# Query and key matmuls in pairs of 256 columns for an even count of instructions, and one remainder visit in the second product

## The chip, the cores and the metric

The kernel runs on one core of one Trainium2 chip. The metric is the device time of one execution in microseconds (us), the median of several runs. A profile is one execution recorded by the hardware profiler; its span is a little shorter than the device time of the same execution.

The engines are named as in the profile: PE is TensorE's matmuls, PEld its weight loads, DVE is VectorE, ACT is ScalarE, POOL is GpSimd, SP is the engine that issues most DMAs. Every matmul here is two TensorE instructions, a weight load and the matmul itself.

## The reference

One transformer layer over x of 2048 rows and 640 columns. First comes an attention that passes a memory from segment to segment, then a feed-forward part; both take a layer norm of their input and add their result to it.

```python
mem = mem0                                    # 8 rows
for s in range(64):                           # segments of 32 rows, one after the other
    h = concatenate([mem, xs[s]])             # 40 rows of 640, xs from layernorm(x)
    q, k, v = h @ Wq, h @ Wk, h @ Wv          # 32 heads of 128
    scores = q @ k.T * 128 ** -0.5            # 40 x 40 a head
    p = softmax(where(mask, scores, -1e9))    # memory rows see all, the others are causal
    o = (p @ v) @ Wo                          # 40 rows of 640
    mem = o[:8]                               # goes into the next segment
    outs.append(o[8:])
h = x + concatenate(outs)
h2 = h + (relu(layernorm(h) @ w1 + b1) ** 2 @ w2 + b2)     # 640 -> 1728 -> 640
```

All arrays are bf16; products accumulate in 32 bits.

## The kernel before

The weights of the attention stay in on-chip memory (`wq`, `wk`, `wv`, `wo`). The order of all instructions is written out by hand: the Python code issues them in the order in which each engine runs them.

**A segment** is one call of `step(b, sp)`. Its 32 "main" rows are the 8 memory rows and 24 of the segment's own rows; the other 8 rows, the "tail", of four segments are projected together ahead of time. The projections go through `proj`: 128 x 32 weights (the transposed rows `hT`) against 512 columns of `wq`, `wk` or `wv`. For each of the five chunks `c` of the 640 inputs, four matmuls `k` = 0 to 3 write the output partitions 32k to 32k + 31 of one PSUM tile, so four of them use the four column groups of the array. A call for one half (`n`) of the heads is 20 matmuls. The order of a segment on TensorE is:

- `project`: queries of half 0, keys of half 0, queries of half 1 (tile `px`), keys of half 1;
- `scores(0)` (L505), the first two chunks of the values of half 0, `token_scores(0)` (L601), the rest of those values, `scores(1)`, `token_scores(1)` and the values of half 1 (tile `px`);
- some work from the list `fill`, `values(0)` (L551, L556: 20 matmuls of 32 or 128 columns), fill, four of the sixteen rounds of the output product (`wo_rounds`, L270, tile `pw`), `values(1)`, the other twelve rounds;
- while ACT and DVE bring the new memory from `pw` into `hT` (`wo_out`, L285 to L287, and `mem_to_hT`, L387): the rest of the fill, and `token_values` of the segment before (L426, L431: 40 matmuls of 32 columns).

`scores(0)` waits for the keys and queries; the first query matmul of the next segment waits for `hT`. `fill` holds the tail projections and the output product of finished tails; `portion` deals them out to the segments, so a segment has between 723 and 771 TensorE instructions, counted from one `scores(0)` to the next.

**The start** (`start`) projects the first tails and the first segment while the weights are still being loaded; `stream` does the queries and then the keys, chunk by chunk.

**The feed-forward part** goes in four passes of 512 rows. The first product (L1008; L1012 for its last, smaller block) makes 1728 = 13 x 128 + 64 hidden columns. The second product (L1060) has four quarters `q` in each pass: row blocks `pr` and `pr + 2`, and half `hf` of the output columns; each quarter is 2 x 13 matmuls of 320 columns. The last 64 hidden columns are the remainder, `rest` (L1037): the row blocks lie in two halves of 64 partitions, so two of its matmuls use two row halves of the array. It is run at the end of quarters 0 and 2, for that quarter and the next. Its tiles come from the pool `yps`; `mm` (three PSUM tiles) serves the first product, and `chn` (one) is free in this part. `y_out` adds the residual on DVE and issues the store.

Of the kernel before, what the change touches and what calls it, by code (L numbers as in the profile page):

```python
# [11 lines left out]
F32 = mybir.dt.float32  # L12
# [4 lines left out]
def kernel(  # L17
# [16 lines left out]
    nc = tc.nc  # L34
    _, S, D = A_x.shape
    _, H, E = A_Wq.shape
    M = A_mem0.shape[1]
    SEG = 32
    G = 4
# [68 lines left out]
    def head(p):  # L108

        n, g, j = p // 16, p // 4 % 4, p % 4  # L110
        return g * HG + j * 2 + n
# [85 lines left out]
    def ln_transpose(b):  # L197
# [23 lines left out]
            nc.scalar.copy(out=rows_in(b).rearrange("p c (s t) -> p c s t", s=4)[:, :, :, 0:HD], in_=ptv[:, :, :, 0:HD])  # L221
        return out

    def proj(w, by, lhs, n, ps, c0, c1):

        if by == "columns":
            wr = w[:].rearrange("p (c g j n k e) -> p c n k g j e", c=DC, g=G, n=2, j=4, k=4)
        elif by == "half":
            wr = w[:].rearrange("p (c k j n e) -> p c n k j e", c=DC, k=G, n=2, j=4)
        else:  # L230
            wr = w[:].rearrange("p (c n g k f) -> p c n k g f", c=DC, n=2, g=2, k=4)
        for c in range(c0, c1):
            for k in range(4):
                nc.tensor.matmul(ps[32 * k:32 * k + 32, :], lhsT=lhs(c), rhs=wr[:, c, n, k], start=(c == 0), stop=(c == DC - 1))  # L234

    def mmtile():
        return mm.tile([128, 512], F32, tag="mm", name="ps")
# [10 lines left out]
    def rowtile():  # L248
        return s2.tile([128, 512], BF16, tag="row", name="row", bufs=4)
# [12 lines left out]
    def wo_rounds(lhs, pw, hs):  # L262

        for h in hs:
            for kh in range(2):
                for ch in range(2):
                    j = kh * 2 + ch
                    p = h // 8 * 16 + kh * 8 + h % 8
                    c0 = 32 * (1 - kh)
                    nc.tensor.matmul(pw[32 * j:32 * j + 32, c0:c0 + DH], lhsT=lhs(p), rhs=wov2[:, head(p), ch],  # L270
                                     start=(h == 0), stop=(h == 15))

    def wo_out(pw, then=None, between=None):
# [145 lines left out]
    def token_values(s, v, vt4, po):  # L419

        sp = s % 4
        pTk, pTx = back.pop()
        for i in range(HG):
            for g in range(G):
                r = slice(32 * g, 32 * g + 32)
                nc.tensor.matmul(po[0][g][:, i * 32:(i + 1) * 32], lhsT=v[r, i * E:(i + 1) * E], rhs=pTk[r, i, :],  # L426
                                 start=(i == 0), stop=False, skip_group_check=True)
        for u in range(2):
            for g in range(G):
                r = slice(32 * g, 32 * g + 32)  # L430
                nc.tensor.matmul(po[0][g][:, u * 128:(u + 1) * 128].rearrange("p (j q) -> p j q", q=32)[:, :, 0:TL],  # L431
                                 lhsT=vt4[r, sp, u, :], rhs=pTx[r, u], start=False, stop=True, skip_group_check=True)

    def token_out(s, po):
# [27 lines left out]
    def step(b, sp, v=None):  # L462
# [11 lines left out]
        def project(which, w, dst, n, between=None):  # L474
            if ready:
                if between:
                    between()
                return
            if which + str(n) == "q1":
                ps = potile(1)  # L480
            elif which + str(n) == "k0" and not last:
                ps = chn.tile([128, 512], F32, tag="ch", name="pk0")[:]
            else:
                ps = mmtile()
            proj(w, "columns", lhs, n, ps, 0, DC)
            row = rowtile()
            if not between:
                evac_row(which, row[:], ps[:])
                flip(row[:], dst, n)
                return  # L490
            for u in range(2):
                nc.scalar.copy(out=row[:, u * 256:(u + 1) * 256], in_=ps[:, u * 256:(u + 1) * 256])  # L492
            between()
            for u in range(2):
                nc.vector.transpose(out=dst[:, n * 16 + u * 8:n * 16 + u * 8 + 8, 0:32],
                                    in_=row[:, u * 256:(u + 1) * 256].rearrange("p (h e) -> p h e", e=32))
# [3 lines left out]
        def scores(n):  # L500
            sm = chn.tile([128, 512], F32, tag="ch", name="sm")
            for j in range(4):
                for g in range(G):
                    p = n * 16 + g * 4 + j
                    nc.tensor.matmul(sm[32 * g:32 * g + 32, 0:NK], lhsT=qz[:, p, :], rhs=kT[:, p, :],  # L505
                                     start=(j == 0), stop=(j == 3), skip_group_check=True)
            sms[n] = sm

# [37 lines left out]
        def values(n, pB, po):  # L546
            cols = po[:, 0, 0:128]
            for j in range(4):
                i = n * 4 + j
                for k in range(4):  # L550
                    nc.tensor.matmul(cols[32 * k:32 * k + 32].rearrange("p (g i m) -> p i g m", g=G, i=4)[:, j],  # L551
                                     lhsT=v[:, i * E + 32 * k:i * E + 32 * k + 32],
                                     rhs=pB[:, :, SEG + j * M:SEG + (j + 1) * M],
                                     start=(j == 0), stop=False, skip_group_check=True)
            for k in range(4):
                nc.tensor.matmul(cols[32 * k:32 * k + 32].rearrange("p (g a) -> p g a", g=G), lhsT=vt4[:, sp, n, 32 * k:32 * k + 32], rhs=pB[:, :, 0:SEG],  # L556
                                 start=False, stop=True, skip_group_check=True)

        def values_out(n, po):
            evac(False, oT[:, n * 16:(n + 1) * 16, SEG:NK], po[:, 0, 0:128].rearrange("p (a m) -> p a m", m=M))  # L560

        project("q", wq, qT, 0)
        if not last and not ready:
            spread(0)
# [32 lines left out]
        def token_scores(n):  # L597
            skv = view()
            for j in range(4):
                for g in range(G):  # L600
                    nc.tensor.matmul(skv[32 * g:32 * g + 32, n * 4 + j, :], lhsT=qT[:, n * 16 + g * 4 + j, :],  # L601
                                     rhs=kT[:, n * 16 + g * 4 + j, :], start=True, stop=True,
                                     skip_group_check=True)

# [208 lines left out]
    def start():  # L813
# [23 lines left out]
        def stream(which, w, dst, turn=None):  # L837
            pas = [pop.tile([128, 2, 512], F32, tag="po%d" % h, name="pa%d" % h) for h in range(2)]
            for c in range(DC):
                for n in range(2):  # L840
                    proj(w, "columns", main, n, pas[0][:, n, :], c, c + 1)
                for n in range(2):
                    proj(w, "columns", lambda c: tail_rows(0, c), n, pas[1][:, n, :], c, c + 1)
                if c == 2 and turn:
                    turn()
                if c < DC - 1:
                    run(units, 7 + c % 2)
            run_late(0, 100)
            for n in range(2):
                row = rowtile()[:]  # L850
                evac_row(which, row, pas[0][:, n, :])
                tail_out(0, which, n, pas[1][:, n, :])
                flip(row, dst, n)
                run_late(0, 100)
                if which == "k":
                    tails_in(0, 0, n)

        stream("q", wq, qT, lambda: ln_transpose(("t", 2))())
        for n in range(2):
            spread(n)  # L860
        tails_v_in(0, nc.gpsimd, 0, 1)
# [133 lines left out]
    for t in range(S // NT):  # L995
# [32 lines left out]
            popx.close()  # L1028
            yps = ctx.enter_context(tc.tile_pool(name="yps", bufs=2, space=bass.MemoryType.PSUM))

        def ytiles():
            return [yps.tile([128, 512], F32, tag="y%d" % hh, name="y%d" % hh) for hh in range(2)]

        def rest(y, pr, cs, first):
            for hh in range(2):
# [14 lines left out]
        for q in range(NK4):  # L1050
            pr, hf = q // 2, q % 2
            cs = slice(hf * DH, (hf + 1) * DH)
            y = y1 if hf else ytiles()
            if more:
                for k in ((0, 1), (2,), (3,), ())[q]:
                    prep_turn(t + 1, k, prep_norm(t + 1, k, hts[k], *mvs[k]))
            for hh in range(2):
                k = pr + 2 * hh
                for fc in range(FFULL):
                    nc.tensor.matmul(y[hh][:, 0:DH], lhsT=f1T[:, fc, k * 128:(k + 1) * 128], rhs=w2[:, fc, cs],  # L1060
                                     start=(fc == 0 and not hf), stop=(fc == FFULL - 1 and hf == 1),
                                     skip_group_check=True)
                if hf:
                    y_out(y, pr, hf, hh)
            if not hf:
                y1 = ytiles()
                rest(y, pr, cs, False)
                rest(y1, pr, slice(DH, D), True)
                for hh in range(2):
                    y_out(y, pr, hf, hh)  # L1070

# [31 lines left out]
```

## Time and profile before

| | us |
|---|---|
| median of 3 runs | 946.59 (945.86 to 948.37) |
| the profiled execution | 946.84 |
| its span | 945.0 |
| PE busy | 918.3 (24,760 matmuls) |
| DVE busy | 681.4 |
| ACT busy | 571.7 |
| POOL busy | 309.7 |

The groups of instructions of the page that the change touches:

| line, what | count | busy us | mean ns |
|---|---|---|---|
| L234 PE, ps from wq, hT | 1260 | 82.7 | 387 |
| L234 PE, px from wq, hT | 1260 | 79.1 | 379 |
| L234 PE, ps from wk, hT | 1280 | 80.2 | 379 |
| L234 PE, pk from wk, hT | 1240 | 78.2 | 380 |
| L1060 PE, y (second product) | 416 | 58.9 | 299 |
| L1037 PE, y (its remainder) | 32 | 3.6 | 301 |

The mean of a matmul is longer than its share of the time, since matmuls overlap: in a stretch of projections, four start together, and the next four 216 ns later. Idle time of an engine that does not carry the end costs nothing. Places in the program are counted in the order in which the built program lists TensorE's instructions.

### The profile page before, as it was taken

How to read it: one execution, taken by the hardware profiler on the slowest of the kernel's cores; microseconds unless marked ns; L12 is line 12 of the kernel's file. 1: busy time of each engine (PE TensorE's matmuls, PEld its weight loads, DVE VectorE, ACT ScalarE, POOL GpSimd, SP SyncE). 2: the span in 40 equal slices, each digit the busy share in tenths (PEclk: the TensorE clock that was granted, in tenths of full speed). 3: DMA queues.
4: the chain of work that ended last, by engine and by line, in shares of the span. 5: the costliest groups of instructions: out<-in, count | busy, mean ns of one | idle time of the engine just before them, and what ended most of it. 6: DMA issues, size and time to landing. Idle time of an engine off the chain costs nothing.

```text
span 945.0 us, 56036 instructions
## 1 busy us (share of the span) xinstructions
PE 918.3 (97%) x24760; PEld 524.0 (55%) x24760; DVE 681.4 (72%) x2068; ACT 571.7 (60%) x1586; POOL 309.7 (33%) x1003
## 2 busy tenths in 40 slices
PE   5979999999999999999999999999999999999998
PEld 2435555655565555555555555565555555565555
DVE  5167887777777777877787787777777788556632
ACT  2446666666666666766676666666666666523321
POOL 2023333333333333333333333333333344344300
PEclk9999999999999999999999999999999999999999
DMA  9982201020102001110101010101010221733320
GB/s 359 408 263 67 45 14 34 9 35 9 22 20 26 19 15 25 20 21 14 32 17 29 9 32 15 32 12 33 15 32 13 53 44 22 233 82 91 91 56 28
DMA packets 65779, 56.66 MB, mean 60 GB/s; under 512 B 37288, under 2 KB 61616, under 8 KB 63616
## 3 DMA queue, kind: packets, MB, share of 16 engines
q1 hardware_dynamic: 65392, 52.74, 20.1%
q8 instruction: 194, 3.18, 1.4%
q14 instruction: 49, 0.40, 0.1%
q0 software_dynamic: 128, 0.33, 0.1%
q10 hardware_dynamic: 16, 0.01, 0.0%
HBM read 38.37 MB, written 9.44 MB: 51 GB/s over the span
## 4 chain that ended last, share of the span: by engine, by line
PE 91%; DMA 4%; SPq 2%; DVE 1%; issue 1%; ACT 1%; DVEq 0%
PE ps L234 23%; PE px L234 21%; PE pw L270 15%; PE pk L234 7%; PE y L1060 6%; PE ps L1008 6%; PE ps L270 3%; PE po L551 2%; DMA wq<-in_A_Wq_dram 2%; PE po L426 2%; SPq L151 2%; PE ps L601 1%; PE sm L505 1%; DMA wo<-in_A_Wo_dram 1%; DMA wv<-in_A_Wv_dram 1%; PE po L556 1%
## 5 line engine op out<-in xcount | busy, mean ns | idle before, releaser
L234 PEld LDWEIGHTS <-hT 128*32 128x32 bf16 x7680 | 180.4, 96 | 160.4 <-DVE hT L387 20.4
L270 PE MATMUL pw<-wo,oT 128*32 128x320 bf16 x4224 | 168.8, 299 | 2.5 <-DMA wo<-in_A_Wo_dram 2.3
L234 PE MATMUL px<-wv,hT 128*32 128x512 bf16 x2520 | 166.0, 377 | 0.0
L270 PEld LDWEIGHTS <-oT 128*32 128x32 bf16 x4224 | 107.7, 96 | 41.6 <-ACT oT L246 19.6
L258 DVE STREAM_TRANSPOSE qT<-row 128x512 bf16<-128x512 bf16 x128 | 89.2, 697 | 36.1 <-ACT row L253 36.0
L679 POOL TENSOR_TENSOR pkt<-ek,rk 128x64 bf16<-128x64 bf16 x64 | 19.0, 296 | 257.0 <-ACT otmp L286 255.4
L234 PE MATMUL ps<-wq,hT 128*32 128x512 bf16 x1260 | 82.7, 387 | 2.7 <-DVE hT L387 2.4
L234 PE MATMUL ps<-wk,hT 128*32 128x512 bf16 x1280 | 80.2, 379 | 0.0
L234 PE MATMUL px<-wq,hT 128*32 128x512 bf16 x1260 | 79.1, 379 | 0.0
L234 PE MATMUL pk<-wk,hT 128*32 128x512 bf16 x1240 | 78.2, 380 | 0.0
L1016 ACT ACTIVATE wv<-ps,b1f 128x512 bf16<-128x512 f32 (+1 forms) x56 | 37.6, 672 | 66.6 <-PE ps L1008 65.7
L437 ACT CAST oT<-po 128x512 bf16<-128x512 f32 x128 | 68.8, 589 | 11.6 <-PE po L431 6.6
L246 ACT CAST oT<-po 128x128 bf16<-128x128 f32 x126 | 33.6, 266 | 63.0 <-PE po L556 58.3
L234 PEld LDWEIGHTS <-hTt 128*32 128x32 bf16 x1920 | 50.7, 96 | 36.2 <-issue 1.7
L451 POOL COPY qz<-qT 128x96 bf16<-128x96 bf16 x126 | 33.6, 267 | 112.7 <-DVE qT L258 112.6
L1060 PE MATMUL y<-wq,wk 128*128 128x320 bf16 x416 | 58.9, 299 | 0.2
L492 ACT CAST row<-ps 128x256 bf16<-128x256 f32 x126 | 40.8, 375 | 29.9 <-PE ps L234 29.9
L253 ACT ACTIVATE row<-ps 128x512 bf16<-128x512 f32 x93 | 54.9, 610 | 6.3 <-PE ps L234 5.1
L253 ACT ACTIVATE row<-px 128x512 bf16<-128x512 f32 x63 | 37.6, 597 | 32.1 <-PE px L234 32.1
L285 ACT COPY otmp<-pw 64x96 f32<-64x96 f32 (+2 forms) x129 | 29.0, 225 | 45.5 <-PE pw L270 23.3
L287 DVE TENSOR_TENSOR o<-pw,otmp 128x96 bf16<-128x96 f32 (+2 forms) x129 | 31.4, 243 | 27.6 <-ACT otmp L286 21.4
L258 DVE STREAM_TRANSPOSE kT<-row 128x512 bf16<-128x512 bf16 x65 | 45.0, 692 | 7.9 <-ACT row L246 7.5
(141 smaller groups left out, 1840.0 us busy)
## 6 DMA issues: line engine op xcount, KB each, us to landing
wv<-in_A_Wv_dram SPq DMA_DIRECT2D x5, 1024.0 KB
wq<-in_A_Wq_dram SPq DMA_DIRECT2D x5, 1024.0 KB
wk<-in_A_Wk_dram SPq DMA_DIRECT2D x5, 1024.0 KB
wo<-in_A_Wo_dram SPq DMA_DIRECT2D x8, 640.0 KB
o_all<-o SPq DMA_DIRECT2D x256, 7.5 KB
vt<-vt_d SPq DMA_DIRECT2D x15, 256.0 KB
xt<-in_A_x_dram SPq DMA_DIRECT2D x19, 160.0 KB
wq<-in_B_w_dram SPq DMA_DIRECT2D x1, 2080.0 KB
```

The lines of the kernel that those rows point to most:

```text
L234: nc.tensor.matmul(ps[32 * k:32 * k + 32, :], lhsT=lhs(c), rhs=wr[:, c, n, k], start=(c == 0), stop=(c == DC - 1))
L246: nc.scalar.copy(out=out_, in_=in_)
L253: nc.scalar.mul(out=row, in_=ps, mul=scale)
L258: nc.vector.transpose(out=dst[:, n * 16:(n + 1) * 16, 0:32], in_=row.rearrange("p (h e) -> p h e", e=32))
L270: nc.tensor.matmul(pw[32 * j:32 * j + 32, c0:c0 + DH], lhsT=lhs(p), rhs=wov2[:, head(p), ch], start=(h == 0), stop=(h == 15))
L287: nc.vector.tensor_tensor(out=five(o[:])[:, cs], in0=blocks(0, 128, 32)[:, cs], in1=five(tmp[:])[:, cs], op=ALU.add)
L437: nc.scalar.copy(out=oTg[:, gs, :, :, 0:SEG], in_=po[1][h][:, :, 0:256].rearrange("p g (n j q) -> p g n j q", n=2, q=32))
L451: nc.gpsimd.tensor_copy(out=d.rearrange("p a (j f) -> p a j f", j=3)[:, :, :, 0:M], in_=src[:, :, 0:3, :])
L492: nc.scalar.copy(out=row[:, u * 256:(u + 1) * 256], in_=ps[:, u * 256:(u + 1) * 256])
L1008: nc.tensor.matmul(ps[:], lhsT=w1[:, c, fc * 128:(fc + 1) * 128], rhs=hnT[:, c, :], start=(c == 0), stop=(c == DC - 1))
L1016: nc.scalar.activation(out=r[:, 0:w], in_=ps[:, 0:w], func=ACT.Relu, bias=b1f[:, fc:fc + 1], scale=1.0)
L1060: nc.tensor.matmul(y[hh][:, 0:DH], lhsT=f1T[:, fc, k * 128:(k + 1) * 128], rhs=w2[:, fc, cs], start=(fc == 0 and not hf), stop=(fc == FFUL ...
```

## The change

Two things.

**Pairs.** `proj` can issue a matmul of 512 columns as two of 256 columns, with the same weights loaded for each, onto the same 32 output partitions. It does so while a counter, `owed`, is above zero, and never in the first or the last of the five chunks. All attention matmuls are counted in `issued`. At the start of each segment's projections the count is compared with a straight line of 1911 / 5 = 382.2 matmuls a segment. What is lacking is made up with pairs: up to 12 in the queries of half 1, then up to 12 in the keys of half 1, then in the keys and queries of half 0. With the waits that stand as instructions of their own, that is 768 TensorE instructions a segment. The queries of the start issue 72 pairs once.

**Remainder.** The second product's `rest` runs for all four quarters at the end of the first quarter, eight matmuls in a row, in place of four at the end of quarters 0 and 2. The output tiles of quarters 2 and 3 are taken from `mm` (three) and `chn` (one). Quarters 1 to 3 finish with their last full block, and `y_out` follows each of their two halves.

```diff
+    issued, owed, paces = [0], [0], []
+
+    def matmul(*args, **kw):
+        issued[0] += 1
+        nc.tensor.matmul(*args, **kw)
+
     def proj(w, by, lhs, n, ps, c0, c1):
...
         for c in range(c0, c1):
             for k in range(4):
-                nc.tensor.matmul(ps[32 * k:32 * k + 32, :], lhsT=lhs(c), rhs=wr[:, c, n, k], start=(c == 0), stop=(c == DC - 1))
+                out_, rhs, start, stop = ps[32 * k:32 * k + 32, :], wr[:, c, n, k], c == 0, c == DC - 1
+                if owed[0] == 0 or start or stop:
+                    matmul(out_, lhsT=lhs(c), rhs=rhs, start=start, stop=stop)
+                    continue
+                owed[0] -= 1
+                for cs, a in ((slice(0, 256), 0), (slice(256, 512), rhs.shape[1] // 2)):
+                    matmul(out_[:, cs], lhsT=lhs(c), rhs=rhs[:, a:a + rhs.shape[1] // 2], start=False, stop=False,
+                           skip_group_check=True)
...
+            owed[0] = extra.pop(which + str(n))
             proj(w, "columns", lhs, n, ps, 0, DC)
+            owed[0] = 0
...
+        extra = {}
+        if not ready:
+            paces.append(issued[0])
+            lack = paces[0] + (1911 * (len(paces) - 1)) // 5 - issued[0]
+            for one in ("q1", "k1", "k0", "q0"):
+                extra[one] = min(max(lack, 0), 12)
+                lack -= extra[one]
         project("q", wq, qT, 0)
...
+        owed[0] = 72
         stream("q", wq, qT, lambda: ln_transpose(("t", 2))())
+        assert owed[0] == 0
...
-        def ytiles():
-            return [yps.tile([128, 512], F32, tag="y%d" % hh, name="y%d" % hh) for hh in range(2)]
+        def ytiles(q):
+            if q < 2:
+                return [yps.tile([128, 512], F32, tag="y%d" % hh, name="y%d" % hh) for hh in range(2)]
+            return [mmtile(), mmtile() if q == 2 else chn.tile([128, 512], F32, tag="ch", name="y3")]
...
-            y = y1 if hf else ytiles()
+            if q == 0:
+                ys = [ytiles(0)]
+            y = ys[q]
...
-                                     start=(fc == 0 and not hf), stop=(fc == FFULL - 1 and hf == 1),
+                                     start=(fc == 0 and q == 0), stop=(fc == FFULL - 1 and q > 0),
                                      skip_group_check=True)
-                if hf:
+                if q:
                     y_out(y, pr, hf, hh)
-            if not hf:
-                y1 = ytiles()
-                rest(y, pr, cs, False)
-                rest(y1, pr, slice(DH, D), True)
+            if q == 0:
+                ys += [ytiles(k) for k in range(1, NK4)]
+                for k in range(NK4):
+                    rest(ys[k], k // 2, slice(k % 2 * DH, (k % 2 + 1) * DH), k > 0)
                 for hh in range(2):
                     y_out(y, pr, hf, hh)
```

The other matmuls of the attention (scores, values, token scores, token values, output product) are issued through `matmul` as well, so that they count.

## The prediction

> **What bounds the kernel now.** I read the page first, then the chain of waits over windows of a few segments, then the timeline where a matmul starts late.
>
> ```profile
> span 945.0 us, 56036 instructions
> PE 918.3 (97%) x24760; PEld 524.0 (55%) x24760; DVE 681.4 (72%) x2068; ACT 571.7 (60%) x1586; POOL 309.7 (33%) x1003
> q8 instruction: 194, 3.18, 1.4%
> PE 91%; DMA 4%; SPq 2%; DVE 1%; issue 1%; ACT 1%; DVEq 0%
> ```
>
> TensorE (PE) carries the end; the clock row of the page is at 9 throughout. The queue that brings instructions moved 194 packets. The program has 49,753 TensorE instructions (24,760 weight loads, 24,760 matmuls, 233 others); over 194 that is 256 each. So TensorE's program arrives in blocks of 256.
>
> One segment closes like this (chain of waits; start, length in us, what):
>
> ```profile
> 405.77 1.67 PE pw L270 x48
> 407.43 0.02 issue
> 407.46 0.24 ACT otmp L285
> ...
> 407.70 0.24 ACT otmp L286
> ...
> 407.97 0.27 DVE o L287
> ...
> 408.26 0.29 DVE hT L387
> 408.55 0.04 issue
> 408.59 1.30 PE ps L234 x20
> ```
>
> The new memory rows go through ScalarE and VectorE for 1.16 us, and only then can the next segment's first query matmul run. TensorE fills that gap with tail work and token values. So a segment is a loop: the matmuls from that query to the last `pw`, then 1.16 us. From the first L505 matmul of one segment to that of the next I measure, over the 58 segments between 79.8 and 771.6 us, 11.93 us on average; 24 of them take 11.77 to 11.79 us, although their fill differs. What lengthens the others looks like this:
>
> ```profile
> 527.42 0.30 PE po L426 x32
> 527.73 0.07 PE po L431 x7
> 527.80 0.78 issue
> 528.58 0.18 PE po L431
> 528.76 1.20 PE ps L234 x20
> ```
>
> "issue" means that no engine and no transfer held TensorE. I put the matmuls' starts beside their places in the program. Between 90 and 760 us fourteen matmuls start over 0.27 us after their columns came free, together 7.1 us. All fourteen stand at place 194 or 195 modulo 256, so at the first instructions of a block. All are in or just behind the dense stretches of small matmuls: values (L551, L556) and token values (L426, L431), where 40 matmuls pass in 0.2 to 0.4 us.
>
> Counting places from a segment's first L505 instruction: segments with a block boundary at 540 to 590 (token values) average 12.17 us (12 of them), at 335 to 400 (second values) 11.96 us (16), the other 30 average 11.81 us. A segment has 723 to 771 instructions, not 768, so its boundaries wander through all places.
>
> **The change part by part.** The order of the changed program gives 25,900 matmuls, so 1,140 pairs: 72 in the start-up and 1,068 in the segments: 22 in the most, none in the fullest. All segments now have 766 to 771 instructions, and the three boundaries stay put: at 195 to 203 (in the second value projection, ahead of the first values), 451 to 459 (end of the `pw` run), and 707 to 715 (start of the second key projection).
>
> *What the pinned boundaries remove.* In the trace of before, a boundary at 684 to 733 delayed its matmul by at most 1 ns (12 cases), one at 427 to 473 by at most 30 ns (15 cases). Nothing falls at 195 to 203: the nearest are 184 and 185 (7 ns) and 212 (107 ns). I take the value near 185, since the wait ahead of the values that lets the queue run dry (place 216 or later) still lies behind the boundary; I keep 0 to 0.1 us for the range. So the 58 segments should come to the 30 segments' mean: 58 x (11.93 - 11.81) = 6.8 us less. Segment 1 had such a stop too, 0.56 us at 71.75 us in the chain of waits: 0.6 us less. The waits on VectorE behind this are not shortened, which is why I go by 11.81 and not by the matmuls' columns: what is late next is the 1.16 us.
>
> *What the pairs cost.* Four matmuls of 32 output rows run side by side on four column groups, a new four every 216 ns (512 columns). On the whole array, 320 columns follow each other in 136 ns (L1060). The two give 0.417 ns a column and 2.7 ns a matmul. A pair on one column group then takes 2 x 109 = 218.7 ns, if the other three groups run meanwhile. In the order of the program they stand behind the pair: first half and second half of group 0, then of group 1. The trace shows whether a matmul of a free group passes one that waits (timeline, TensorE):
>
> ```profile
> 616.13 0.40 PE L505 MATMUL sm<-kT,qz 128*32 128x40 bf16 x10
> 616.35 0.39 PE L234 MATMUL px<-wv,hT 128*32 128x512 bf16 x2
> 616.36 0.25 PE L505 MATMUL sm<-kT,qz 128*32 128x40 bf16 x6
> ```
>
> All 16 `sm` matmuls stand ahead of the `px` ones in the program, yet two `px` start before the last six `sm`. After a stop at 611.5 us two groups had fallen a round behind; the other two went through their four `sm` matmuls and were up to eleven matmuls ahead. A four of pairs asks for five. So I take 2.7 ns for each four pairs: 267 x 2.7 = 0.7 us, 0.8 with fours that are split in part. All of it is on the loop, as the pairs are in the second query and key projections; the added weight loads run beside matmuls (PEld is 55% busy). The lower bound is 0; the upper, if order held, is 55 ns a pair (below).
>
> The Trainium skill, "TensorE: Matmul & The Clock Gate", Part 3, The mechanism, says that matmuls start and end strictly in program order and only weight loads are pulled ahead. By that rule the pairs would cost the upper bound; the timeline above disagrees with it.
>
> The 72 pairs of the start-up cost 18 x 2.7 ns, under loads: there the chain runs through the transfers of `wq` and `wo` until 59.56 us. If that cover were gone it is 0.05 us.
>
> *The remainder of the second product.*
>
> ```profile
> 836.22 3.64 PE y L1060 x26
> 839.85 0.38 PE y L1037 x4
> 840.23 7.17 PE y L1060 x52
> 847.40 0.38 PE y L1037 x4
> ```
>
> A visit to the remainder holds four matmuls in two row halves: 2 x 136 = 272 ns of work in 0.38 us, 0.11 over; the 52 matmuls behind it take 0.10 over their 52 x 0.136. The change makes one visit of eight in place of two of four, in each of four passes: 4 x 0.2 = 0.8 us less. The accumulators of the last two quarters now come from `mm` and `chn`, which the next pass's first product uses. Its first tile was freed in the third quarter, its third one by the addition after the first half of the last quarter, 1.8 us before the pass ends; I cost this at nothing. If the cover were gone it is one addition, about 0.5 us, three times. The last output's path (additions and stores of the last quarter) is unchanged. No DMA, no ScalarE, GpSimd or VectorE instruction is added or moved past another.
>
> Sum: -6.8 - 0.6 + 0.8 - 0.8 = -7.4 us. The profiled execution took 946.84 us (span 945.0), so 939.4; the median of the three runs is 0.25 lower: 939.2 us.
>
> **Rivals.**
>
> *The pairs run in order (slower), 8%.* Each second half would hold up the next group's first half: four pairs take 4 x 109 = 436 ns in place of 216, 55 ns a pair; 1,068 x 55 = 58.7 us. With the gains of 8.2 us: 946.6 + 58.7 - 8.2 = 997 us. It decides from 8.2 us / 1,068 = 7.7 ns a pair on. Against it stands the timeline at 616 us; for it, that no row shows two matmuls in a row on one column group of four, so passing within pairs is carried over from another case.
>
> *The boundary at 195 to 203 stalls (slower), 4%.* The block before it gets shorter, about 3.1 us, as split projections hold more instructions in the same time. If it then comes as late as those at the token values, 12.17 - 11.81 = 0.36 us in each of 60 segments: 939.2 + 21.6 = 961 us. Against it: five blocks of 3.0 us in before (ending at 118.1, 213.0, 308.9, 499.4 and 691.6 us) delayed nothing over 11 ns.
>
> *The stops stay (no change), 6%.* They would come from something else than block boundaries and fall elsewhere; then -0.8 + 0.8 leaves 946.6 us. All fourteen places speak against it.
> The Trainium skill, "Runtime: NRT & Kernel Launch", Instruction fetch mechanics, says the crossing of a 256-instruction block is mostly hidden, which would give this result; the 0.78 us stop above disagrees, though most boundaries here do agree.
>
> **How the numbers follow.** The forecast, 939.2 us, has 82%. Its own bounds: all segments at 11.78 us (1.8 us less) and free pairs (0.8) give 936.6, and the runs spread 0.7 below their median, so 936.0; 0.1 us lost at each boundary at 195 to 203 gives 945. So 936.0 to 945.0, which leaves out the three rivals, 18%. A measurement of this kernel tells 0.3% (2.8 us) from no change: the forecast lies under 943.8 in 79 of its 82, the other 3 go with the 6 of "the stops stay" to no change, 12% is slower.
>
> **What would show it.** Right: segments of 11.78 to 11.83 us; no "issue" stops over 0.3 us at L426, L431, L551 or L556 (their new line numbers); a four of pairs as eight 128x256 matmuls whose next four starts 219 ns after it; remainder visits of eight in 0.65 us. Wrong: 436 ns for a four of pairs and segments near 12.8 us (order holds); "issue" ahead of the first values in most segments (the boundary stalls); stops at other places than the first instructions of a block.

## The result, and the profile of the changed kernel

The changed kernel takes 944.24 us (median of 22 runs, 940.0 to 947.3) against 947.68 us (945.86 to 949.77) for the kernel before in the same comparison. The ratio is 0.9963, with a 95% interval of 0.9952 to 0.9973: 3.4 us less, where the prediction had 7.4. The execution that was profiled took 947.3 us, the longest of the 22, so its own stretches must be compared with care.

The page of the changed kernel (span; busy time of each engine; the queue that brings instructions; the chain that ended last, by engine):

```profile
span 945.5 us, 58317 instructions
PE 921.6 (97%) x25900; PEld 558.7 (59%) x25900; DVE 681.9 (72%) x2068; ACT 571.0 (60%) x1586; POOL 309.2 (33%) x1003
q8 instruction: 203, 3.33, 1.5%
PE 91%; DMA 4%; SPq 2%; DVE 1%; ACT 1%; issue 0%; POOL 0%; DVEq 0%
```

The 1,140 pairs are there: 25,900 matmuls in place of 24,760. The program has 52,033 TensorE instructions, and 203 packets of the instruction queue, where there were 194: one for each block of 256, as before. TensorE still carries the end.

Three views say that the prices of the pairs and of the remainder were right. First the timeline of TensorE in one segment (start, length in us, then the group; groups overlap):

```profile
361.39 1.26 PE L228 MATMUL ps<-wq,hT 128*32 128x512 bf16 x20
362.48 1.25 PE L228 MATMUL pk<-wk,hT 128*32 128x512 bf16 x20
363.56 1.26 PE L228 MATMUL px<-wq,hT 128*32 128x512 bf16 x32
364.64 0.39 PE L228 MATMUL ps<-wk,hT 128*32 128x512 bf16 x4
```

The third line is a projection with twelve pairs, 32 matmuls. It takes 1.08 us from its start to the start of the next, as the plain one of 20 matmuls above it does (362.48 to 363.56). Start by start, the first halves of four pairs begin within some 10 ns of one another (411.970 to 411.980 us in one four), the second halves 109 ns later, and the next four 218 ns after the first (median of 143), where four plain matmuls take 216. Second, the remainder (timeline again):

```profile
840.75 0.44 PE L1088 MATMUL y<-wq,wk 128*128 128x320 bf16 x2
841.11 0.45 PE L1063 MATMUL y<-wq,wk 64*128 64x320 bf16 x4
841.40 0.43 PE L1063 MATMUL ps<-wq,wk 64*128 64x320 bf16 x3
841.53 0.30 PE L1063 MATMUL y<-wq,wk 64*128 64x320 bf16 x1
841.76 1.13 PE L1088 MATMUL y<-wq,wk 128*128 128x320 bf16 x7
```

Its eight matmuls start at 841.11 and the next block follows at 841.76, 0.65 us later. The four passes of the second product, measured from the start of their first matmul to the start of their last, shrink from 14.97, 15.22, 15.22 and 14.97 us to 14.76, 15.01, 15.01 and 14.76: 0.85 us in all. Third, the stop of segment 1 at 71.75 us is gone; the chain of waits runs on from matmul to matmul there.

What did not come is the gain of the pinned boundaries. One segment closes like this (chain of waits, the changed kernel; start, length, what):

```profile
371.00 0.68 PE pw L228 x20
371.68 0.54 issue
372.22 0.59 PE pw L228 x11
372.81 0.79 PE ps L228 x22
```

The first matmul at 372.22 us stands at place 453 of its segment, behind the boundary of a block. The profile names nothing that it waits for. I call "late" the time by which a matmul starts after its columns of the array came free. In segments 2 to 59, the 58 of the prediction, this is what the three boundaries of the profiled execution did:

| boundary at | late on average | late by over 0.11 us | most |
|---|---|---|---|
| 195 to 203 | 0.023 us | 5 of 58 | 0.304 us |
| 451 to 459 | 0.133 us | 26 of 58 | 0.838 us |
| 707 to 715 | 0.000 us | 0 of 58 | 0.001 us |

The third boundary lies among pairs. There the starts must be set against the places half by half, since the program lists both halves of one column group before the next group, while the trace has the four first halves start together. Set in the program's order, one half seems 0.10 us late and another seems to start 0.10 us before its columns are free. That 0.10 us stands at the same places in the other kernels with pairs, wherever their boundaries lie, and e7 below, which lists the halves in the order of their starts, has none of it; it is no delay. I count blocks as late from 0.11 us on.

The 58 segments take 692.08 us (11.932 each), against 691.86 (11.929) in the profiled execution of before. The 18 of them under 11.80 us average 11.785; the 24 of before averaged 11.781. So an undisturbed segment is as short as it was, and the time above that, 58 x 0.147 = 8.5 us here, goes with the late blocks, whose lateness at the first two boundaries adds up to 58 x 0.156 = 9.0 us. Most of it shows as "issue" nowhere, since another column group still runs while one is late: the waits of PE name only 1.5 us at `pw`, in four stops.

### The profile page after: what moved, and what is told of

The parts are those of the page before. It is cut to its first block, busy times and chain, and to the rows that moved or that the text cites. A ratio compares the mean times of both kernels' runs of the same rounds, so it can differ in the third digit from the quotient of the medians.

```text
span 945.5 us, 58317 instructions
## 1 busy us (share of the span) xinstructions
PE 921.6 (97%) x25900; PEld 558.7 (59%) x25900; DVE 681.9 (72%) x2068; ACT 571.0 (60%) x1586; POOL 309.2 (33%) x1003
## 4 chain that ended last, share of the span: by engine, by line
PE 91%; DMA 4%; SPq 2%; DVE 1%; ACT 1%; issue 0%; POOL 0%; DVEq 0%
PE ps L228 28%; PE px L228 22%; PE pw L228 15%; PE pk L228 7%; PE ps L1032 6%; PE po L228 5%; PE y L1088 3%; PE ps L1088 2%; DMA wq<-in_A_Wq_dram 2%; SPq L151 2%; PE sm L228 1%; DMA wo<-in_A_Wo_dram 1%; DMA xt<-in_A_x_dram 1%; DVE wk L1041 0%; DVE lnst L158 0%
## 5 line engine op out<-in xcount | busy, mean ns | idle before, releaser
L228 PEld LDWEIGHTS <-hT 128*32 128x32 bf16 x8764 | 212.5, 96 | 134.1 <-DVE hT L400 20.3
L228 PE MATMUL pw<-wo,oT 128*32 128x320 bf16 x4224 | 170.9, 300 | 3.7 <-issue 1.5
L228 PE MATMUL ps<-wk,hT 128*32 128x512 bf16 (+1 forms) x1695 | 80.2, 327 | 0.0
L228 PE MATMUL px<-wq,hT 128*32 128x512 bf16 (+1 forms) x1895 | 79.3, 308 | 0.0
L228 PE MATMUL pk<-wk,hT 128*32 128x512 bf16 (+1 forms) x1252 | 78.3, 379 | 0.0
L228 PEld LDWEIGHTS <-v 32*128 32x128 bf16 (+1 forms) x4064 | 47.7, 93 | 51.4 <-issue 43.3
L228 PEld LDWEIGHTS <-hTt 128*32 128x32 bf16 x1976 | 55.3, 97 | 36.2 <-issue 6.3
L510 DVE STREAM_TRANSPOSE kT<-row 128x256 bf16<-128x256 bf16 x126 | 48.6, 424 | 2.9 <-ACT row L507 0.2
```

The lines of the kernel that those rows point to most:

```text
L228: nc.tensor.matmul(*args, **kw)
```

## The experiments

Two stretches are read in each trace: the 58 segments, and the lateness at each boundary. The three boundaries of a segment sit where the number of start-up pairs puts them, so changing that one number moves all of them together and leaves everything else in the segments alone.

| kernel | boundaries at | median us | ratio to before (95%) | 58 segments, us |
|---|---|---|---|---|
| changed | 195–203, 451–459, 707–715 | 944.24 | 0.9963 (0.9952–0.9973) | 692.08 |
| e1 remainder only | as before | 946.97 | 1.0003 (0.9989–1.0018) | 693.52 |
| e2 pairs only | as changed | 944.84 | 0.9981 (0.9966–0.9996) | 688.35 |
| e3 start 41 | 1–9, 257–265, 513–521 | 939.14 | 0.9921 (0.9903–0.9938) | 685.48 |
| e4 start 21 | 41–49, 297–305, 553–561 | 953.92 | 1.0075 (1.0057–1.0092) | 700.79 |
| e5 start 92 | 155–163, 411–419, 667–675 | 941.28 | 0.9949 (0.9933–0.9965) | 687.51 |
| e9 start 84 | 171–179, 427–435, 683–691 | 938.89 | 0.9936 (0.9917–0.9955) | 687.50 |
| e10 start 50 | 239–247, 495–503, 751–759 | 938.09 | 0.9931 (0.9909–0.9953) | 685.45 |
| e6 start 41, old second product | as e3 | 939.07 | 0.9930 (0.9912–0.9947) | 685.07 |
| e7 start 41, halves apart | as e3 | 937.84 | 0.9920 (0.9903–0.9937) | 685.28 |
| e8 48 pairs a segment | not pinned | 973.74 | 1.0295 (1.0270–1.0321) | 714.98 |
| e11 waits later | as changed | 956.69 | 1.0113 (1.0087–1.0138) | 701.99 |
| e12 waits sooner | as changed | 951.42 | 1.0062 (1.0038–1.0087) | 698.26 |

The column of segments is of one execution each; medians and ratios are of all.

**The two parts alone.** e1 is the kernel before with only the new second product, e2 the changed kernel with the old one.

```diff
 # e1: before.py with the new ytiles(q) and rest(...) for all four quarters; no pairs
 # e2: after.py with the old ytiles() and rest(...) in quarters 0 and 2
```

> The kernel before with the second product's change alone (one remainder visit of eight a pass, no pairs). Theory A (what is left of the gain is lost again to stops at the first instructions of a block, now at the places 451 to 459, because a block is used up there before the next one has come): the remainder is worth what its rows say, 4 x 0.2 = 0.8 us, so 0.5 to 1.0 us under before, ratio 0.999 to 0.9995. Theory B (the remainder cost more than its cover allowed, by the tiles taken from mm and chn, and that ate the gain): 1 to 4 us over before.

> The changed kernel with the second product as before (pairs alone). Theory A: 0.8 us over the changed kernel, so about 2.7 us under before, ratio 0.997. Theory B: 1 to 4 us under the changed kernel, ratio 0.992 to 0.995.

e1 is at 1.0003: the 0.85 us that the trace shows in the passes is a tenth of a per cent, inside its interval. e2 carries what there is of gain, 0.9981, and its interval overlaps that of the whole change. The remainder is not where the missing 4 us went. e2 is also a second profiled execution with the changed kernel's boundaries (943.33 us): at 451 to 459 the average lateness was 0.049 us there, with 12 blocks of 58 late. So this boundary is not late every time, which goes with the wide scatter of the changed kernel's runs (940.0 to 947.3).

**The boundaries moved.** Only the number of pairs in the start changes.

```diff
-        owed[0] = 72
+        owed[0] = 41      # e3; 21 in e4, 92 in e5
```

> The changed kernel with 41 pairs in the start in place of 72. All boundaries move 62 places on, to 1-9, 257-265 and 513-521; nothing else moves. In the trace of before no boundary at 1-11, 256-267 or 512-523 delayed a matmul over 10 ns. Theory A: hardly any stop, segments of 11.78 to 11.82 us, 939 to 941 us, ratio 0.991 to 0.994. Theory C (each fetched block costs the same on average, wherever its boundary lies): as the changed kernel, ratio 0.996 to 0.997.

> The changed kernel with 21 pairs in the start. Boundaries move to 41-49, 297-305 and 553-561, the last in the token values of every segment. Theory A: the segments take what those of before with a boundary at 540-590 took, 12.17 us, 0.36 us over the others: 20 us over e3, 955 to 962 us, ratio 1.008 to 1.016. Theory C: as the changed kernel, ratio 0.996 to 0.997.

> The changed kernel with 92 pairs in the start: boundaries at 155-163, 411-419 and 667-675. In the traces so far the fetch of the next block begins 1.2 to 1.3 us after a boundary (median) where a wait that stands as an instruction of its own follows within 34 places, and 0.6 to 0.7 us after it where the first such wait is 35 to 50 places on; in the changed kernel it stands 13 to 40 places behind the boundary at 195-203. Theory D (the fetch of a block is asked for some way into the block before it, and a wait ahead of that point holds it back): now the wait is 53 or more places off, the fetch begins by 0.7 us, and the boundary at 411-419 stops in few segments: 939 to 941 us, ratio 0.992 to 0.994. Theory A2 (only the time in which a block is used up counts): the block from 155 to 411 is no longer than the one from 195 to 451, so the stops stay or grow: 944 to 947 us, ratio 0.997 to 1.000.

From 939.14 to 953.92 us, in one comparison: 14.8 us hang on where the boundaries fall. With 41, the average lateness at the three is 0.009, 0.016 and 0.025 us, and the gain is 0.79%, 7.5 us, the size that was forecast for the change as drawn; its segments average 685.48 / 58 = 11.82 us, and the prediction had 11.81. With 21, the kernel is a little under the 955 to 962 us that were expected. The last boundary falls into the token values; its block is late in 33 of 58 segments, by 0.323 us on average over all 58 and by up to 1.02 us (chain of waits, e4):

```profile
170.87 0.62 PE ps L228 x16
171.49 0.30 PE po L228 x32
171.79 0.85 issue
172.65 0.22 PE po L228 x8
172.87 1.18 PE ps L228 x17
```

This is the kind of stop that the kernel before showed at L431, now in most segments. The same stretch of e3, where no boundary falls, has a segment's end without it:

```profile
368.28 0.92 PE ps L228 x24
369.20 0.30 PE po L228 x32
```

e5 lies between, and neither of its expected ranges holds: its block at 411 to 419 is late in 9 of 58 segments, with the packet at 0.78 us (median) and a shorter block than the changed kernel's, 3.55 us against 3.79 without the lateness.

**Is it the pairs?** e6 is e3 with the old second product. e7 is e3 with the halves of four groups issued as four first halves, then four second halves, so that no two matmuls in a row are on one column group. e8 always splits twelve in each of the four projections: 48 pairs and 831 instructions a segment, with nothing to pin the boundaries.

```diff
 # e7, in proj:
-                for cs, a in ((slice(0, 256), 0), (slice(256, 512), rhs.shape[1] // 2)):
-                    matmul(out_[:, cs], lhsT=lhs(c), rhs=rhs[:, a:a + rhs.shape[1] // 2], ...)
+                matmul(out_[:, 0:256], lhsT=lhs(c), rhs=rhs[:, 0:mid], ...)
+                halves.append((out_[:, 256:512], rhs[:, mid:]))
+            for out_, rhs in halves:
+                matmul(out_, lhsT=lhs(c), rhs=rhs, ...)
 # e8, in step:
-                extra[one] = min(max(lack, 0), 12)
-                lack -= extra[one]
+                extra[one] = 12
```

> e3 (41 pairs in the start) with the second product as before, so the remainder's part alone, in a kernel whose runs spread less. The remainder saves what its rows say: 0.8 us over e3, 939.9 us. If it costs or gives nothing: 939.1 us.

> e3 with the halves of a four of pairs written apart: the first halves of the four column groups, then the second halves, so that no matmul stands behind one that waits for its own group. Theory: groups pass each other, so the order in which a pair is written costs nothing: as e3, 939.1 us within 0.7. Rival (order holds in part and pairs in a row lose time): faster than e3 by up to 0.055 us x 1,068 = 59 us if it held in full.

> The changed kernel with 48 pairs in every segment (12 in each of the four query and key projections), not paced: 831 instructions a segment, boundaries that wander. Theory: a four of pairs costs 2.7 ns, so 48 x 60 / 4 x 2.7 ns = 1.9 us for the matmuls; the rest is the supply of instructions: 3.25 blocks in 11.8 us, 3.63 us for each, while the blocks that made no stop lasted 3.0 us or more and those that stopped up to 3.9 us. 952 to 975 us, ratio 1.005 to 1.03. Rival (order holds, 55 ns a pair): 2,880 x 0.055 = 158 us more, 1,100 us.

e7's interval lies on e3's, so the order of the halves is worth nothing that can be measured: a second half does not hold up the next group, as the starts above say too. e6 equals e3 too; here as in e1 the remainder's 0.85 us stays inside the intervals. e8 costs 2.95%, about 27 us. If order held, some 2,800 pairs (48 in 58 segments) at the prediction's 55 ns would have cost 153 us. What e8 does pay shows at all kinds of matmuls, with no engine named (waits of PE, e8: what waited for what, us in total, times, longest):

```profile
PE po L228 <- issue: 5.9, 17, 0.6
PE ps L228 <- issue: 5.1, 8, 1.6
PE pw L228 <- issue: 3.5, 10, 0.7
PE px L228 <- issue: 3.0, 8, 0.7
```

Its segments take 12.327 us and hold 831 / 256 = 3.25 blocks: 12.327 / 3.25 = 3.8 us a block. The changed kernel has three blocks in a segment, 3 x 3.8 = 11.4 us, inside the 11.785. So blocks can be had fast enough on average, and what counts is when each is asked for.

**When a block is asked for.** I took the packets of the instruction queue in order and set each against the boundary of its block. A packet takes 1.04 us (median over the ten kernels below), and no block that was late by over 0.11 us began less than 1.21 us after its packet ended. The packet itself starts some time after the boundary before. That time goes with how far behind that boundary the next wait stands that is an instruction of its own on TensorE. Over the kernels before, changed, e2 to e5 and e9 to e12:

| next such wait | boundaries | packet starts after the boundary (median) | late by over 0.11 us |
|---|---|---|---|
| under 35 places on | 304 | 1.27 us | 102 |
| 35 to 59 | 213 | 0.76 us | 7 |
| 60 to 99 | 221 | 0.78 us | 10 |
| 100 or more | 992 | 0.46 us | 28 |

Blocks of like length give the same picture: of those whose own work took 3.4 to 4.0 us, 58 of 192 were late in the first row, 20 of 449 in the other three together.

In the changed kernel the wait ahead of the first values stands 13 to 40 places (median 18.5) behind the boundary at 195 to 203. The packet for the block at 451 to 459 started 1.25 us after it, and 1.25 + 1.1 + 1.2 to 1.5 = 3.6 to 3.9 us, while the work of that block takes 3.8. In the nine segments where the packet started within 0.7 us, no block was late; of the 47 where it started after 1.0 us, 26 were.

Two starts were meant to tell this from the other reading, that only the time of the block decides. e9's boundary at 427 to 435 ends a block of 3.77 us, as short as the changed kernel's, but its wait is 37 or more places off; e10's is farther still.

```diff
-        owed[0] = 72
+        owed[0] = 84      # e9; 50 in e10
```

> The changed kernel with 84 pairs in the start: boundaries at 171-179, 427-435 and 683-691, so the wait ahead of the first values (place 216 in most segments) stands 37 places or more behind the first boundary; in the changed kernel it stood 13 or more. Theory D (a wait within some 34 places behind a boundary holds back the fetch of the next block): the fetch begins 0.6 to 0.8 us after the first boundary, not 1.25, and at 427-435 at most 10 of 58 segments stop over 0.1 us (26 in the changed kernel): 940 to 942 us, ratio 0.993 to 0.995. Theory A2 (only the time in which the block is used up counts, and it is no longer here): 944 to 946 us, ratio 0.997 to 0.999.

> The changed kernel with 50 pairs in the start: boundaries at 239-247, 495-503 and 751-759. The first now lies behind the wait ahead of the first values and some 66 places ahead of the next one (313). Theory D: the fetch begins by 0.5 us after that boundary, few stops at 495-503; 939 to 941.5 us, ratio 0.992 to 0.9945. Theory A2: the block from 239 to 495 takes no longer than the one from 195 to 451, so stops as in the changed kernel: 944 to 946 us.

They came out at 938.89 and 938.09 us. In e9 the packet started 0.76 us after the boundary (median) and the block was late in 4 of 58 segments, not 26, at nearly the same time per block. The reading by block time alone does not hold. That rests on e9: e10's block from 239 to 495 took 4.15 us, longer than its expectation had it, so that both readings let it be in time. It has 2 late blocks at 495 to 503, though its packet started there at 0.97 us with the wait 66 or more places off, later than the table has it for such distances.

**Only the wait moved.** The last two keep all boundaries and move the wait, by running more of the fill, or none of it, ahead of the first values.

```diff
-            run(fill, (ahead - 1) // 2, held, True)
+            run(fill, ahead, held, True)      # e11; 0 in place of ahead in e12
             values(0, pT0, po[1][0])
```

> The changed kernel with its block boundaries where they are (195 to 203, 451 to 459, 707 to 715); more of the fill is run ahead of the first values, so that the wait that stands as an instruction of its own lies 13 to 72 places behind the boundary at 195 to 203 (median 38) in place of 13 to 40 (median 18.5). If a wait close behind a boundary holds back the request for the next block: in the segments whose wait lies 35 or more places off (about half), the fetch starts 0.6 to 0.7 us behind the boundary and the matmul at 451 to 459 is late by 0.03 us or less; in the others it starts at 1.2 to 1.3 us and the delay stays at some 0.13 us; the mean falls to about 0.07 us and the kernel takes 58 x 0.06 = 3.5 us less than the changed one, about 941 us. If only the place of the boundary, and so the time of the block, counts: the fetch and the delays are alike in near and far segments, the mean stays at 0.13 us and the time at 944 us.

> The same boundaries; no fill ahead of the first values, so that the wait lies 5 to 13 places behind the boundary at 195 to 203 in every segment. If a wait close behind a boundary holds back the request: no segment has the fetch early, and the mean delay at 451 to 459 is 0.13 us or more; 944 to 948 us. If only the place counts: 0.13 us and 944 us, as in the changed kernel. The first values now stand earlier and may wait for the softmax; a wait of TensorE there would show in the trace at the values and not at 451 to 459.

In e11 the boundary at 451 to 459 did what was expected, within one execution:

| e11, wait behind the boundary at 195 to 203 | segments | packet starts | late by over 0.1 us | average lateness |
|---|---|---|---|---|
| under 34 places | 23 | 1.17 us | 6 | 0.087 us |
| 34 or more | 35 | 0.60 us | 0 | 0.0002 us |

The time did not: 956.69 us where 941 was expected. All of that fill now runs ahead of the first values, which leaves nothing between them and the four rounds of the output product that need them, and TensorE waits for ScalarE's copy (e11: waits of PE, then the chain of waits in one segment):

```profile
PE pw L228 <- ACT oT L259: 13.3, 40, 0.5
```

```profile
120.34 0.20 PE po L228 x16
120.54 0.02 issue
120.56 0.27 ACT oT L259
120.83 0.04 issue
120.88 0.73 PE pw L228 x16
```

In the changed kernel that wait is 0.4 us in all. The waits list only the times in which all of TensorE stood still; counted by the columns, those rounds start late in 46 of the 58 segments, by 19.4 us in all. The lateness at 195 to 203 and at 451 to 459 falls by 6.8 us, and the 58 segments are 9.9 us longer than in the changed kernel. The wait also lengthens the blocks of the far segments (4.15 us against 3.92 in the changed kernel), but this is not why most of them were in time: from the end of the packet to the boundary they had 2.45 us (median), and without the wait, 0.49 us there on average, 1.9 us, and over 1.6 in 32 of the 35, where late blocks began 1.2 to 1.6 us after their packet.

In e12 the wait stands 5 to 13 places on, the packets start at 1.30 us, and 10 of 58 blocks are late at 451 to 459, 0.065 us on average, half of the 0.13 us that was expected at least. The total of 951.42 us was not expected either. The first values now stand ahead of the softmax's end, and the chain of waits passes through VectorE and ScalarE in each segment, as here:

```profile
366.89 0.77 DVE kT L510 x2
...
368.16 0.26 DVE pT L553
368.41 0.02 issue
368.44 0.25 ACT pB L556
368.69 0.02 issue
368.70 0.39 ACT em L531 x2
369.10 0.34 PE po L228 x20
```

No segment is under 11.91 us any more. The blocks take 3.94 us in place of 3.80, which leaves more room for the packet; that fewer are late goes with it. So e11 shows the stop going with the wait, in segments of one kernel; e12 shows the late packets, with fewer stops under them.

What stays open: why a wait close behind a boundary puts the packet off. The trace has the ends of these waits: in the changed kernel the wait behind 195 to 203 ended 0.07 to 0.35 us after the boundary and the packet started 1.08 us after that end (median; half of them 0.91 to 1.15), in e12 1.10 us. In e9, with the wait farther on, the packet started only 0.20 us after its end. A request that the near wait holds and the far one does not would fit this, but no view shows the request. Nor is there a run with the wait moved and nothing else late.

## Why the prediction was right or wrong

**What was right.** TensorE's program comes in blocks of 256, and the long segments are late blocks: e3 and e4 differ only in the pairs of the start, and so in the boundaries' places, and lie 14.8 us apart. The pairs are nearly free as matmuls: four of them take 218 ns in the trace, where the prediction had 219; e7, where no second half stands right behind its first, is not measurably faster than e3, and the undisturbed segments grew by 0.004 us, where the prediction had up to 22 / 4 x 2.7 ns = 0.015. The rival "the pairs run in order" is out by the starts, e7 and e8. So is the rule that the prediction set beside it, from the Trainium skill, "TensorE: Matmul & The Clock Gate", Part 3, The mechanism, that matmuls start and end in program order: by it e8 would have paid the 153 us. The remainder's 0.8 us came as 0.85 in the trace, though no comparison of times resolves it. Segment 1's 0.6 us came. And "a boundary at 684 to 733 delayed its matmul by at most 1 ns" carried over: at 707 to 715 nothing was later than that.

**The step that failed** is "What the pinned boundaries remove", in the part on the boundary at 451 to 459: "one at 427 to 473 by at most 30 ns (15 cases)". It made 6.8 us out of 58 segments of 11.81. In the profiled execution, the slowest, the boundary cost 133 ns on average and up to 838, and the segments were 11.93; in e2's faster one it cost 49 ns and they were 11.87. Over all runs the gain was about half of the forecast. I judged a boundary by its own place alone. A block's chance to be in time depends on the packet's start, and so on what lies behind the boundary before. Pinning fixes both: with 195 to 203 as the boundary before, the wait ahead of the first values is always 13 to 40 places on, and the packet 0.5 us later. In the kernel before, none of the 15 rows lies at 451 to 459: eleven are at 427 to 441, where the boundary before has the same wait 31 to 48 places off and the packet started at 0.7 us in seven, and four at 468 to 473, where that wait stands 4 places on or less, or is past. So rows to both sides stood for a gap between them, and the wait lies differently in the gap. That is not the whole of it: in six of the 15 the packet started as late as in the changed kernel, at 1.25 to 1.54 us, and none of the six was over 29 ns late, where 26 of 47 were in the changed kernel. Why those six were in time stays open. The prediction used that wait only to argue that the boundary at 195 to 203 itself would not be late (0.023 us, which was near enough).

**Range and rivals.** The measured 944.24 us lies inside the range of 936.0 to 945.0, but by luck: the upper end stood for 0.1 us lost at each boundary at 195 to 203, which lost 0.023, and the time went to the boundary that was put at nothing. The rival "boundary at 195 to 203 stalls" did not happen at its own place, but its mechanism, a pinned place that is bad in most segments, happened one boundary later, and e4 is what it looks like in full: 953.92 us, a ratio to before of 1.0075 against the changed kernel's 0.9963. "The stops stay" is out, since the stops follow the boundaries in every run. The Trainium skill, "Runtime: NRT & Kernel Launch", Instruction fetch mechanics, which the prediction named beside this rival, says that the next block is fetched while the current one runs; the packets agree, with starts at 0.46 to 1.27 us after the boundary before (the medians above). It also says that the crossing is mostly hidden: that holds for most boundaries here, and fails where a block's work takes about 3.8 us and its packet starts at 1.25 us.

With the same pairs and another start the forecast of 7.4 us is met: e3 gains 0.79% (0.62 to 0.97), e10 0.69% (0.47 to 0.91). The sum was right for a benign place of the boundaries; the price of this one place was wrong.

## What to carry to other kernels

Where a TensorE-bound loop is a whole number of instruction blocks long, the place of the block boundaries in the loop is a parameter of its own: e3 and e4 took 939 and 954 us here at the same work in the loop, and a few split instructions ahead of the loop set it, so it is cheap to try several. Judge a place by the time from the boundary before to it, and by what stands just behind the boundary before; here a wait that is an instruction of its own within 34 places behind it went with late blocks (102 of 304, and 45 of 1,426 elsewhere). A row of the old trace speaks for a new fixed place only if what lies around it is the same too.

## What the runs showed of the hardware

- A block of 256 TensorE instructions takes a packet of about 1.04 us; a late block began 1.2 to 1.6 us after the end of its packet in most cases; and e8, with 12.327 us for 3.25 blocks, had one every 3.8 us. If that is the limit of supply, an instruction there costs 3.8 us / 256 = 15 ns, where a pair's second half cost some 0.5 ns as a matmul (four pairs took 218 ns, four plain matmuls 216).
- The packet of a block starts 0.46 to 0.78 us after the boundary before it (medians), and 1.27 us after it where a wait that is an instruction of its own stands within 34 places.
- A late block is mostly not seen as idle TensorE: the profiled execution of the changed kernel lost 8.5 us in its segments, and the waits of PE list 1.5 us as "issue". Starts set against places in the program show the rest.
- Matmuls on free column groups start ahead of earlier ones in the program: of four pairs listed group by group, the four first halves start within some 10 ns of one another and the second halves 109 ns later.
